# Two phase seams of a fused backward kernel, re-laid: the last output row sums, and the first two rows of the w2 gradient

## The chip, the cores and the metric

The kernel runs on one core of a Trainium2 chip. The metric is the device time of one execution in microseconds (us), the median of several runs. Five engines work side by side, each through its own queue in order: TensorE (PE, matmuls), VectorE (DVE), ScalarE (ACT), GpSimd (POOL) and SyncE (SP), the last used here only to issue DMA transfers; POOL issues transfers as well.

## The reference, cut to what matters

The reference is the forward pass of a block and all its gradients (a vector-Jacobian product with `grad_out`). The block takes tokens `x` (2048 x 1024), normalizes and modulates them, mixes them by a two-dimensional FFT with a learned spectrum, normalizes again, and applies an MLP of width 3584:

```python
def _B_ref(x, w1, b1, w2, b2):
    y = _layernorm(x, axis=-1)
    h = _gelu(jnp.einsum('bsd,df->bsf', y, w1) + b1)
    return jnp.einsum('bsf,fd->bsd', h, w2) + b2
x = A_x
mod = (_silu(c) @ w_mod).reshape(c.shape[0], 6, 1, -1)
sa, ca, ga, sb, cb, gb = (mod[:, 0].copy(), ..., mod[:, 5].copy())
h = _layernorm(x, axis=-1) * (1 + ca) + sa
x = x + ga * _A_ref(h, A_w_r, A_w_i)
h = _layernorm(x, axis=-1) * (1 + cb) + sb
x = x + gb * _B_ref(h, B_w1, B_b1, B_w2, B_b2)
return x
...
_out, _vjp = jax.vjp(_f, A_x, A_w_r, A_w_i, B_w1, B_b1, B_w2, B_b2, c, w_mod)
_grads = _vjp(grad_out)
```

Three results matter here. The gradient of `gb` is the sum over all tokens of `grad_out` times the MLP's output; it is the last of six rows that feed the gradient of `w_mod`. The gradient of the MLP's input is the product of the gradient before the activation with `w1` transposed. The gradient of `w2` is the product of the hidden activations, transposed, with `grad_out * gb`, summed over tokens.

## The kernel before, in words

The kernel works through phases, one after another on TensorE, and the tile framework plans the order of each engine's queue ahead of time: it goes by the order in the program, by when it expects inputs and buffers to be ready, and by the marks `tc.high_priority()` (sooner) and `tc.issue_after(ins)` (the instructions of this block that run on the engine of `ins` stand behind it). Buffers with one tag share a place: a later tile of the tag waits until the earlier one is no longer read. PSUM has eight banks of 128 x 512, in three pools: `ps_s` (two banks), `ps_d` (two) and `ps_f` (four).

**The forward MLP** (lines 762 to 881) runs over four blocks of 512 tokens (`b`), in an order written out by hand (`plan`). `z_block` makes the hidden activations and their gradient factors and stores them to `d_hh` and `d_gz`. `bo_pass(b, h)` makes one column half `h` of the output of a block: 112 matmuls into four banks (`pbo`), evictions on ACT, then on DVE the product `go * bo` and the output itself (`otile` holds these, and the tag is `ot`). After that it yields, and its remainder sums the product over tokens: four `pa` matmuls, added by DVE to `gacc`. The last pass, b = 3 and h = 1, keeps its sums in `ps_s` and `ps_d`; its remainder runs right behind the plan (lines 879 and 880), and `store_gmod` (line 881) writes `gacc` to the DRAM row 5 of `d_gmod`.

**The input gradient** (lines 977 to 1030) runs over the same blocks. For each, SP loads `n3u`, `n2u`, the tokens of `grad_out` into `got` (tag `ot`, half of it by POOL's indirect loads) and seven groups of `d_gz` into a ring of eight slots (`gzr`). For each column half, 112 `pg` matmuls go into the four `ps_f` banks, seven weight groups of sixteen. ACT evicts them, and a chain on DVE and ACT (`ln_bwd`, products, sums, `fold_tok`, `fold_d`) makes that block's part of `fbuf2`. Column sums of intermediate results go to TensorE again (`sums3`, `sums3_ga`, into `acc3`). The ring `early` works the row 5 of the modulation gradient through in eight steps: load a block of `w_mod`, two DVE instructions, store; its first `next` loads the row from `d_gmod` and the first two blocks of `w_mod`.

**The w2 gradient** starts behind it. Four tiles `gB0` to `gB3` hold `grad_out` of a token block each, scaled by `gb` on DVE; they take the places of the weight tiles `w1T_0` to `w1T_3`. `pieces()` is a generator whose steps are spread over later phases by `fill(n)`. For each of 28 rows `fc` of 128 hidden channels it loads the activations by a transposing DMA (`hh_load`), and for each column half adds up 16 matmuls, four on each `gB`, into one `ps_f` bank:

```python
        hh_load(0)
        yield
        hh_load(1)
        for fc in range(NFC):
            if fc + 2 < NFC:
                hh_load(fc + 2)
            for h in range(2 if fc < NFC - 2 else 0):
                acc = ps_f("gw2acc")
                for t in range(NT):
                    gw2_mm(acc, fc, h, t)
                gw2_out(acc, fc, h)
                yield
```

Lines 1173 to 1179 run sixteen of these steps ahead of the spectral backward pass: the first `next` issues row 0's load, then `fill(6)` stands behind the last `gB` load on SP, then come the last block's column sums (`sums3(3, ...)`) and `fill(10)`. The spectral pass then begins with `s_fwd` (the `pu` matmuls), which reads all four parts of `fbuf2`.

Of the kernel before, what the change touches and what calls it, by code (L numbers as in the profile page):

```python
# [11 lines left out]
BF16 = mybir.dt.bfloat16  # L12
I32 = mybir.dt.int32
ACT = mybir.ActivationFunctionType
ALU = mybir.AluOpType
AX = mybir.AxisListType

P = 128
S = 2048
D = 1024  # L20
# [3 lines left out]
NFC = F // P  # L24
KH = D // 2
# [5 lines left out]
NB = 4  # L31
# [4 lines left out]
def kernel(  # L36
# [89 lines left out]
    def load_tok(t4, src, i, eng=None):  # L126
        s3 = tok_flat(src)
        ins = (eng or nc.sync).dma_start(out=t4[:, 0:4:3, :],
                          in_=bass.AP(tensor=s3.tensor, offset=s3.offset + 128 * i * D, ap=[[D, P], [1024 * D, 2], [1, D]]))
        for q in range(2):  # L130
            nc.gpsimd.indirect_dma_start(out=t4[:, 1 + q, :], out_offset=None, in_=s3,
                                         in_offset=bass.IndirectOffsetOnAxis(ap=xidx[:, 2 * i + q:2 * i + q + 1], axis=0))
        return ins
# [38 lines left out]
    def tt(out, a, b, op):  # L172
        return nc.vector.tensor_tensor(out=out, in0=a, in1=b, op=op)  # L173

    def store_gmod(srcs, r):
        row = small.tile([1, D], BF16, tag="gmrow", bufs=1)
        for h in range(2):
            nc.vector.tensor_copy(out=row[:, h * KH:(h + 1) * KH], in_=srcs[h])
        nc.sync.dma_start(out=d_gmod[r * D:(r + 1) * D].rearrange("(o n) -> o n", o=1), in_=row[:])
# [623 lines left out]
    def bo_pass(b, h):  # L803
        cs_ = slice(h * KH, (h + 1) * KH)
        pbs = [(ps_f if b < NB - 1 or h == 0 else (ps_s, ps_d)[k % 2])("pbo") for k in range(4)]
        for i in range(4):
            with ordered():
                last_pe[0] = nc.tensor.matmul(pbs[i][:], lhsT=ones_bf[0:1, :], rhs=b2_row[0:1, cs_], start=True, stop=False)
        for g in range(7):
            wp = w2p[w2n[0] % 4]  # L810
            w2n[0] += 1
            nc.sync.dma_start(out=wp, in_=w2_v[:, g * 4:(g + 1) * 4, cs_])
            hh = hh_slots[(b * 7 + g) % 11]
            for i in range(4):
                for k in range(4):
                    with ordered():
                        last_pe[0] = nc.tensor.matmul(pbs[i][:], lhsT=hh[:, k, i * P:(i + 1) * P], rhs=wp[:, k, :],  # L817
                                                      start=False, stop=(g == 6 and k == 3))
            if g < 6:
                yield  # L820
        bo, x1t, go = (otile[0][:, k] for k in range(3))
        nc.sync.dma_start(out=x1t, in_=chunk_rows(d_x1, b)[:, :, cs_])
        load_tok_half(go, grad_out, b, h)
        for i in range(4):
            with tc.high_priority():
                last_ev[0] = nc.scalar.copy(out=bo[:, i, :], in_=pbs[i][:])
        tt(go, go, bo, ALU.mult)
        tt(bo, bo, bcn(gb_row[:, cs_], 4), ALU.mult)
        tt(bo, bo, x1t, ALU.add)
        store_tok_half(out_0, bo, b, h)  # L830

        yield
        pa = (ps_d if b < NB - 1 else ps_f)("pa")
        for i in range(4):
            with ordered():
                last_pe[0] = nc.tensor.matmul(pa[:], lhsT=ones_bf[:], rhs=go[:, i, :], start=(i == 0), stop=(i == 3))
        with tc.high_priority():
            if b == 0:
                nc.vector.tensor_copy(out=gacc[:, cs_], in_=pa[0:1, :])  # L839
            else:  # L840
                tt(gacc[:, cs_], gacc[:, cs_], pa[0:1, :], ALU.add)
# [19 lines left out]
    for kind, b, g in plan:  # L861
# [7 lines left out]
        else:  # L869
# [6 lines left out]
                bo_late.clear()  # L876
            if g == 13:
                next(boq[b], None)
    for late in bo_late:
        next(late, None)  # L880
    store_gmod([gacc[:, 0:KH], gacc[:, KH:D]], 5)

    gb1 = small.tile([P, NFC], FP32, tag="gb1", bufs=1)
    nc.vector.reduce_sum(out=gb1[:], in_=gb1_acc[:], axis=AX.X)
    gb1_bf = small.tile([P, NFC], BF16, tag="b1_bf", bufs=1)
# [67 lines left out]
    n3u = reg.tile([P, 4, D], BF16, name="n3u", tag="uv1")  # L953
    n2u = reg.tile([P, 4, D], BF16, name="n2u", tag="uv2")
    pru = reg.tile([P, 4, D], BF16, name="pru", tag="uv3")[:]
    got = reg.tile([P, 6, D], BF16, name="got", tag="ot")
    fbuf2 = reg.tile([P, 4, 4, D], BF16, name="fbuf2", tag="fr")
    acc3 = [ps_d("acc3a"), ps_d("acc3b")]
    gzn = 0
    gmw = reg.tile([P, 2, D], BF16, name="gmw", tag="ph")  # L960
    gmg = reg.tile([P, 2, D], BF16, name="gmg", tag="sb")
    early = gmod_ring((5,), [gmw[:, 0], gmw[:, 1], gmg[:, 0]], gmg[:, 1, :])
    next(early)
    au = reg.tile([P, 4, D], BF16, name="au", tag="px1")

    fold2_in = {}

# [9 lines left out]
    for b in range(NB):  # L977
        gn3 = gn3s[b % 2]
        sums = small.tile([P, 2, 4], FP32, tag="sums")
        gzt = []  # L980
        nc.sync.dma_start(out=n3u[:], in_=chunk_rows(d_n3, b))
        nc.sync.dma_start(out=n2u[:], in_=chunk_rows(d_x1, b))
        norm_act(n2u, n2u, 1, b)
        go4 = got[:, 0:4, :]
        load_tok(go4, grad_out, b)
        for g in range(7):
            sl = gzr[gzn % 8 // 2][:, gzn % 2]
            gzn += 1
            nc.sync.dma_start(out=sl, in_=d_gz_v[:, g * 4:(g + 1) * 4, b * BW:(b + 1) * BW])
            gzt.append(sl)  # L990
        for h in range(2):
            pgs = [ps_f("pg") for _ in range(4)]
            for g in range(7):
                for i in range(4):
                    for k in range(4):
                        nc.tensor.matmul(pgs[i][:], lhsT=gzt[g][:, k, i * P:(i + 1) * P],  # L996
                                         rhs=w1Ts[g][:, k, h * KH:(h + 1) * KH],
                                         start=(g == 0 and k == 0), stop=(g == 6 and k == 3))
            for i in range(4):
                with tc.high_priority():  # L1000
                    nc.scalar.activation(out=gn3[:, i, h * KH:(h + 1) * KH], in_=pgs[i][:], func=ACT.Identity,
                                         accum_out=sums[:, h, i:i + 1])
        tt(sums[:, 0, :], sums[:, 0, :], sums[:, 1, :], ALU.add)
        for i in range(4):
            t = 4 * b + i
            ln_bwd(gn3[:, i, :], sums[:, 0, i:i + 1], n3u[:, i, :], stats[:, 2, 0, t:t + 1], gn3[:, i, :], got[:, 4 + i % 2, :])
        next(early, None)
        tt(pru, gn3[:], n2u[:], ALU.mult)
        g2, ftmp = gn3, pru
        if b < NB - 1:  # L1010
            sums3(b, gn3, pru)
        else:
            g2, ftmp = gn3s[0], gzr[0].rearrange("p a b (c d) -> p (a b c d)", c=1).rearrange("p (q d) -> p q d", d=D)
        s2c = small.tile([P, 4], FP32, tag="s2c")
        for i in range(4):
            t = 4 * b + i
            nc.vector.tensor_tensor_reduce(out=g2[:, i, :], in0=gn3[:, i, :], in1=opcb_row, scale=1.0, scalar=0.0,
                                           op0=ALU.mult, op1=ALU.add, accum_out=s2c[:, i:i + 1])
            ln_bwd(g2[:, i, :], s2c[:, i:i + 1], n2u[:, i, :], stats[:, 1, 0, t:t + 1], g2[:, i, :], got[:, 4 + i % 2, :])
        next(early, None)  # L1020
        tt(g2[:], g2[:], go4, ALU.add)
        nc.gpsimd.dma_start(out=chunk_rows(d_gx1, b), in_=g2[:])
        nc.sync.dma_start(out=au[:], in_=chunk_rows(d_A, b))
        tt(n3u[:], g2[:], bcn(ga_row, 4), ALU.mult)
        fold_tok(n3u, ftmp)
        fold2_in[b] = fold_d(fbuf2[:, b], n3u[:], ftmp)
        tt(au[:], g2[:], au[:], ALU.mult)
        if b < NB - 1:
            sums3_ga(b, au)
            next(early, None)  # L1030
# [58 lines left out]
    def gw2_mm(acc, fc, h, t):  # L1089
        nc.tensor.matmul(acc[:], lhsT=hh_s[hh_o[fc]][:, t, :], rhs=gBs[t // 4][:, t % 4, h * KH:(h + 1) * KH],  # L1090
                         start=(t == 0), stop=(t == NT - 1))
# [21 lines left out]
    def pieces():  # L1113
        def hh_load(fc):
            hh_in[0] = nc.sync.dma_start_transpose(out=hh_s[hh_o[fc]], in_=d_hh[fc * P:(fc + 1) * P, :])

        hh_load(0)
        yield
        hh_load(1)
        for fc in range(NFC):  # L1120
            if fc + 2 < NFC:
                hh_load(fc + 2)
            for h in range(2 if fc < NFC - 2 else 0):
                acc = ps_f("gw2acc")
                for t in range(NT):
                    gw2_mm(acc, fc, h, t)
                gw2_out(acc, fc, h)
                yield
# [39 lines left out]
    def fill(n):  # L1168
        for _ in range(n):
            next(todo)  # L1170
        done[0] += n

    next(todo)
    with tc.issue_after(gb_in.ins):
        fill(6)
    for cl in (CE, SE, CO, SO):
        nc.sync.dma_start(out=(smA2, smB2)[cl % 2][:, cl // 2], in_=d_SF[:, cl])
    sums3(3, gn3s[1], pru)
    fill(10)
    nc.sync.dma_start(out=em2, in_=d_E[:, 0])  # L1180

    def mid_bwd():
# [74 lines left out]
```

## Time and profile before

| what | value |
|---|---|
| median of 4 runs | 1523.47 us (1519.96 to 1535.19) |
| profiled execution, its own time | 1524.67 us |
| profiled execution, span | 1522.5 us |
| TensorE busy | 1433.5 us (94%), 6697 matmuls |
| DVE busy | 1073.1 us (70%) |
| ACT busy | 722.5 us (47%) |
| POOL busy | 363.4 us (24%) |
| mean granted TensorE clock | 0.982 |
| DRAM traffic | 324.27 MB by DMA, mean 213 GB/s |

The profile comes from one execution. Its own time holds the span (first to last instruction) and what lies around it. Engine shares are averages over the whole span. The granted clock is the share of its full clock that TensorE was given. In listings by order of time, a line has the start in us, the length in us, the engine, the program line, the operation, the output and inputs, and in brackets how long the engine was idle before and what ended that. SPq is the queue of DMA issues on SP; the length there is the time of the issue, not of the transfer.

### The profile page before, as it was taken

What the parts mean: (1) busy time and instruction counts of PE and PEld (TensorE: products, weight loads), DVE (VectorE), ACT (ScalarE), POOL (GpSimd) and SP (SyncE); (2) the same over time, 40 slices, a digit from 0 to 9 for tenths busy, and PEclk for the clock granted to TensorE, in tenths of its full rate; (3) what the DMA queues carried; (4) which work ended last, traced back from release to release, by engine and by line L of the source; (5) the groups of instructions that cost most, each with busy time, mean ns of one, the idle gap of its engine ahead of it and who ended that gap; (6) DMA issues with size and microseconds to landing.
All of it is one profiled execution on the core that took longest, in us unless ns stands there. A gap on an engine that the chain in (4) does not pass through costs nothing.

```text
span 1522.5 us, 18221 instructions
## 1 busy us (share of the span) xinstructions
PE 1433.5 (94%) x6697; PEld 668.7 (44%) x6831; DVE 1073.1 (70%) x1577; ACT 722.5 (47%) x956; POOL 363.4 (24%) x428
## 2 busy tenths in 40 slices
PE   5989899999999999999999999979998899999998
PEld 2434445444444444444434444434444444444443
DVE  5992869897799887877224977967066666898642
ACT  4765556668886666656012333322522344443211
POOL 5720621211113122221111101311033421222422
PEclk9999999999999999999999999989999999999999
DMA  9871744989587886899956336496288986766992
GB/s 327 270 218 42 203 157 160 284 261 340 198 259 243 198 265 232 243 280 263 335 173 213 132 104 221 110 276 174 63 198 225 235 251 174 199 172 165 275 280 103
DMA packets 358160, 324.27 MB, mean 213 GB/s; under 512 B 209187, under 2 KB 300849, under 8 KB 357816
## 3 DMA queue, kind: packets, MB, share of 16 engines
q1 hardware_dynamic: 324184, 207.71, 51.4%
q0 software_dynamic: 33888, 115.41, 22.1%
q8 instruction: 53, 0.87, 0.2%
q14 instruction: 35, 0.29, 0.1%
HBM read 164.15 MB, written 109.10 MB: 179 GB/s over the span
## 4 chain that ended last, share of the span: by engine, by line
PE 50%; DVE 21%; issue 9%; DMA 9%; ACT 6%; POOL 2%; SPq 1%; POOLq 0%; ACTq 0%; DVEq 0%
PE pbo L817 11%; PE gw2acc L1090 10%; PE pz L776 9%; PE pg L996 5%; PE pv L544 4%; DVE ct L173 4%; PE pu L451 3%; PE pp L659 2%; PE gw1acc L1157 2%; DVE got L895 2%; DVE fbuf L173 1%; DMA xt<-d_gx 1%; DMA gB<-in_grad_out_dram 1%; DMA wblk<-in_w_mod_dram 1%; DVE gn3a L900 1%
## 5 line engine op out<-in xcount | busy, mean ns | idle before, releaser
L659 PE MATMUL pp<-gBoT,wt 128*128 128x512 bf16 x874 | 199.0, 381 | 3.2 <-ACT pho L669 1.0
L996 PE MATMUL pg<-w1T,gzr 128*128 128x512 bf16 x884 | 195.8, 380 | 1.1
L1157 PE MATMUL gw1acc<-gzh,n3n 128*128 128x512 bf16 x875 | 195.6, 380 | 1.1
L776 PEld LDWEIGHTS <-w 128*128 128x128 bf16 x896 | 87.6, 98 | 109.0 <-issue 3.6
L996 PEld LDWEIGHTS <-gzr 128*128 128x128 bf16 x896 | 88.0, 98 | 107.6 <-issue 3.1
L659 PEld LDWEIGHTS <-wt 128*128 128x128 bf16 x896 | 87.8, 98 | 104.1 <-issue 3.1
L1157 PEld LDWEIGHTS <-n3n 128*128 128x128 bf16 x896 | 87.8, 98 | 103.8
L776 PE MATMUL pz<-n3Tb,w 128*128 128x512 bf16 x439 | 98.7, 379 | 1.9 <-DVE w2sD L839 1.5
L776 PE MATMUL pz<-n3Ta,w 128*128 128x512 bf16 x440 | 98.2, 379 | 1.9 <-ACT gt L779 1.3
L1090 PE MATMUL gw2acc<-gB,hhsA 128*128 128x512 bf16 x438 | 98.9, 379 | 0.5
L817 PEld LDWEIGHTS <-hhA 128*128 128x128 bf16 x608 | 59.7, 99 | 77.9 <-issue 9.3
L1095 ACT CAST gwo<-gw2acc 128x512 bf16<-128x512 f32 x54 | 30.6, 584 | 121.9 <-PE gw2acc L1090 76.5
L779 ACT ACTIVATE gt<-pz,b_col 128x512 bf16<-128x512 f32 x112 | 72.9, 684 | 29.7 <-PE pz L776 26.0
L785 ACT ACTIVATE gt<-gt 128x2048 bf16<-128x2048 bf16 x28 | 53.4, 1910 | 64.1 <-DVE gt L173 64.0
L173 DVE TENSOR_TENSOR gt<-gt,gt 128x2048 bf16<-128x2048 bf16 x56 | 68.4, 1222 | 15.9 <-ACT gt L787 15.1
L1161 ACT CAST gwo<-gw1acc 128x512 bf16<-128x512 f32 x48 | 27.8, 584 | 108.2 <-PE gw1acc L1157 100.1
L173 DVE TENSOR_TENSOR ct<-ct 128x2048 bf16<-128x2048 bf16 x64 | 76.0, 1219 | 0.8
L1090 PE MATMUL gw2acc<-gB,hht 128*128 128x512 bf16 x250 | 58.4, 391 | 9.6 <-DVE gB L173 9.1
L1090 PEld LDWEIGHTS <-hhsA 128*128 128x128 bf16 x448 | 43.9, 98 | 50.4
L781 ACT ACTIVATE gt<-gt 128x2048 bf16<-128x2048 bf16 x28 | 53.5, 1910 | 7.6 <-DVE gb_acc L796 6.9
L787 ACT ACTIVATE gt<-gt 128x2048 bf16<-128x2048 bf16 x28 | 53.3, 1908 | 0.4
L1162 POOL DMA_DIRECT2D out_dram<-gwo x56 | 30.5, 547 | 86.7 <-ACT gwo L1161 58.5
(314 smaller groups left out, 2552.4 us busy)
## 6 DMA issues: line engine op xcount, KB each, us to landing
gzr<-d_gz SPq DMA_DIRECT2D x28, 512.0 KB, 7.3
wblk<-in_w_mod_dram SPq DMA_DIRECT2D x12, 1024.0 KB, 13.3
d_ph<-pho POOLq DMA_DIRECT2D x21, 512.0 KB, 5.4
out_dram<-otl POOLq DMA_DIRECT2D x40, 256.0 KB, 3.6
d_hh<-hhA POOLq DMA_DIRECT2D x19, 512.0 KB, 5.1
w2sD<-in_B_w_dram SPq DMA_DIRECT2D x14, 512.0 KB, 6.3
hhC<-d_ph SPq DMA_DIRECT2D x14, 512.0 KB, 5.2
w2sA<-d_ph SPq DMA_DIRECT2D x14, 512.0 KB, 5.1
```

Of the source, the lines that this page charges most:

```text
L173: return nc.vector.tensor_tensor(out=out, in0=a, in1=b, op=op)
L544: nc.tensor.matmul(pv[:], lhsT=R[:, cl * 4 + m, :, :].rearrange("p x w -> p (x w)")[:, base:base + 255:2], rhs=smi[:, cl // 2, m, :], star ...
L659: last_pe[0] = nc.tensor.matmul(pp[:], lhsT=wt[:, fg % 2, cch, k * P:(k + 1) * P], rhs=gBoT[j][:, cch, :], start=(cch == 0), stop=(cch == ...
L776: last_pe[0] = nc.tensor.matmul(pz[:], lhsT=w1s[g][:, cch, k * P:(k + 1) * P], rhs=n3T[:, cch, :], start=(cch == 0), stop=(cch == NDC - 1))
L779: nc.scalar.activation(out=zb[:, k, :], in_=pz[:], func=ACT.Identity, bias=b1_col[:, fc:fc + 1], scale=1.0)
L781: nc.scalar.activation(out=av, in_=zb, func=ACT.Square)
L785: nc.scalar.activation(out=sg, in_=bv, func=ACT.Sigmoid, scale=2.0 * GK)
L787: nc.scalar.activation(out=bv, in_=bv, func=ACT.Sigmoid, scale=-2.0 * GK)
L817: last_pe[0] = nc.tensor.matmul(pbs[i][:], lhsT=hh[:, k, i * P:(i + 1) * P], rhs=wp[:, k, :], start=False, stop=(g == 6 and k == 3))
L996: nc.tensor.matmul(pgs[i][:], lhsT=gzt[g][:, k, i * P:(i + 1) * P], rhs=w1Ts[g][:, k, h * KH:(h + 1) * KH], start=(g == 0 and k == 0), sto ...
L1090: nc.tensor.matmul(acc[:], lhsT=hh_s[hh_o[fc]][:, t, :], rhs=gBs[t // 4][:, t % 4, h * KH:(h + 1) * KH], start=(t == 0), stop=(t == NT - 1))
L1157: nc.tensor.matmul(acc[:], lhsT=n3ns[t // 4][:, t % 4, cch * P:(cch + 1) * P], rhs=gz2[t // 8][:, t % 8, :], start=(t == 0), stop=(t == NT ...
```

## The change: what it does

At the first seam, the remainder of the last `bo_pass`, the store of row 5, the first step of `early` and the tiles `got` and `au` move from before the input gradient to between the matmuls of its first half (b = 0, h = 0) and that half's evictions. The load of `got` for block 0 moves with them. The last `pa` uses the pool `ps_s` instead of `ps_f`.

At the second seam, rows 0 and 1 of the w2 gradient are made together, token block by token block, with four accumulators in two pools. The load of row 1 is issued before the first yield, and the column sums of the last block come after eight pieces instead of six.

```diff
-        pa = (ps_d if b < NB - 1 else ps_f)("pa")
+        pa = (ps_s if b == NB - 1 and h == 1 else ps_d if b < NB - 1 else ps_f)("pa")
...
-    for late in bo_late:
-        next(late, None)
-    store_gmod([gacc[:, 0:KH], gacc[:, KH:D]], 5)
-
...
-    got = reg.tile([P, 6, D], BF16, name="got", tag="ot")
...
-    next(early)
-    au = reg.tile([P, 4, D], BF16, name="au", tag="px1")
...
-        go4 = got[:, 0:4, :]
-        load_tok(go4, grad_out, b)
+        if b > 0:
+            load_tok(got[:, 0:4, :], grad_out, b)
...
+            if b == 0 and h == 0:
+                for late in bo_late:
+                    next(late, None)
+                store_gmod([gacc[:, 0:KH], gacc[:, KH:D]], 5)
+                next(early)
+                got = reg.tile([P, 6, D], BF16, name="got", tag="ot")
+                au = reg.tile([P, 4, D], BF16, name="au", tag="px1")
+                load_tok(got[:, 0:4, :], grad_out, b)
...
-        tt(g2[:], g2[:], go4, ALU.add)
+        tt(g2[:], g2[:], got[:, 0:4, :], ALU.add)
...
         hh_load(0)
+        hh_load(1)
         yield
-        hh_load(1)
         for fc in range(NFC):
             if fc + 2 < NFC:
                 hh_load(fc + 2)
-            for h in range(2 if fc < NFC - 2 else 0):
+            if fc == 1:
+                first = [(f_, h, (ps_s, ps_f)[f_]("gw2acc")) for f_ in range(2) for h in range(2)]
+                for b in range(NB):
+                    for f_, h, acc in first:
+                        for t in range(4 * b, 4 * b + 4):
+                            gw2_mm(acc, f_, h, t)
+                    if b < NB - 1:
+                        yield
+                for f_, h, acc in first:
+                    gw2_out(acc, f_, h)
+                yield
+            for h in range(2 if 1 < fc < NFC - 2 else 0):
...
     with tc.issue_after(gb_in.ins):
-        fill(6)
+        fill(8)
...
     sums3(3, gn3s[1], pru)
-    fill(10)
+    fill(8)
```

## The prediction

> **What bounds the kernel now.** I read the page first, then the table of who waited for whom on TensorE over 700 to 1100 us, then the order of time on each engine at the two places the change touches, then the stretches there.
>
> ```profile
> span 1522.5 us, 18221 instructions
> PE 1433.5 (94%) x6697; PEld 668.7 (44%) x6831; DVE 1073.1 (70%) x1577; ACT 722.5 (47%) x956; POOL 363.4 (24%) x428
> ```
>
> TensorE is busy for 94% of the span, so time is won only where it stands still or runs slowly. Its waits:
>
> ```profile
> PE gw2acc L1090 <- DVE gB L173: 9.1, 3, 5.1
> PE pa L836 <- DVE otile L173: 3.6, 1, 3.6
> PE acc3a L193 <- DVE au L173: 2.9, 3, 1.0
> ```
>
> The columns are total, times and longest, in us. The two largest are the two seams of the change. Seam one, between the last output pass and the input gradient, in order of time (start, length, engine, line):
>
> ```profile
> 775.26 0.23 PE L188 MATMUL ptr<-fin,gb_bf 128*28 128x128 bf16 x1
> 779.11 1.79 PE L836 MATMUL pa<-otile,ones_bf 128*128 128x512 bf16 x4 [3.62 <-DVE otile L173]
> 780.69 53.14 PE L996 MATMUL pg<-w1T,gzr 128*128 128x512 bf16 x236
> ```
>
> Four column-sum matmuls wait for DVE's product, and the pg matmuls, whose operands are there, stand behind them. Seam two, where the w2 gradient starts:
>
> ```profile
> 997.78 1.03 PE L1090 MATMUL gw2acc<-gB,hht 128*128 128x512 bf16 x4
> 1000.69 1.02 PE L1090 MATMUL gw2acc<-gB,hht 128*128 128x512 bf16 x4 [1.88 <-DVE gB L173]
> 1006.79 1.87 PE L1090 MATMUL gw2acc<-gB,hht 128*128 128x512 bf16 x4 [5.08 <-DVE gB L173]
> 1010.78 3.57 PE L1090 MATMUL gw2acc<-gB,hht 128*128 128x512 bf16 x8 [2.13 <-DVE gB L173]
> 1014.58 16.43 PE L1090 MATMUL gw2acc<-gB,hht 128*128 128x512 bf16 x74 [0.22 <-issue]
> ```
>
> Each arriving token block gives four matmuls of work, then TensorE waits for the next. The blocks come late because of what SP queues and how full the DMA engines are:
>
> ```profile
> 975.13 0.42 SPq L128 DMA_DIRECT2D gB<-in_grad_out_dram  x1
> 975.60 8.22 SPq L1115 DMA_TRANSPOSE hht<-d_hh  x1
> 983.91 0.53 SPq L128 DMA_DIRECT2D gB<-in_grad_out_dram  x1
> 988.12 10.02 SPq L128 DMA_DIRECT2D gB<-in_grad_out_dram  x1
> 998.19 14.36 SPq L1115 DMA_TRANSPOSE hht<-d_hh  x3
> ```
> ```profile
> 1000.00:1010.00 10.00, 2.89 (x8) 0.89 (x8) 4.49 (x3) 0.00 (x0) 1.53 (x1) 0.73 1.13 297
> ```
>
> The last three numbers are granted clock, DMA share and GB/s. The transfers fill the DMA engines, and TensorE runs at clock 0.73 besides waiting.
>
> **Seam one, step by step.** The pa matmuls, DVE's two casts, the row store and the start of the gmod ring move behind the 112 matmuls of the first half (b = 0, h = 0). From the end of ptr (775.49) to the first pg (780.69) are 5.20 us; the four pa come back later at 0.2157 each (112 matmuls of the half take 24.17 us, read from the first evictions of the two halves, 803.44 and 827.61), 0.86. That leaves 4.3. The first half also ran slowly: its first eviction should follow the first pg after 100 matmuls and some 0.2 us, at 802.4, and came at 803.44: 1.0 lost to the clock after the gap. Gain 4.3 to 5.3; I take **5.0**, since no gap is left. The eight gzr loads that pg needs first were issued by 743, and pg's four banks were free. pa takes a bank of pool s, which is idle after ptr, so that edit costs nothing; without it pa would wait for one of pg's four banks.
>
> What is late next: the pa matmuls now end at 775.5 + 24.17 + 0.86 = 800.5. DVE's add and cast wait for them; DVE had only ring steps until 828, so they cover. On SP the moved issues are the row store, the load of the gradient row, the ring's first loads, got and au. In before the row load follows pa's end (780.9) by 4.2 us, so now it comes at 804.7; from that load to the ring's last product took 785.06 to 816.7, 31.6 us, so the ring ends near 836, while DVE's chain for b = 0 starts at 828.3 - 5.0 = 823.3. If every ring step stood ahead of that chain, it and the first column sums behind it on TensorE would be up to 13 us late; if the steps slip into DVE's 7.5 us gap before each later chain (932.7 to 940.2 is one), nothing. The nearest row is TensorE's wait for a DVE product in this stage, 1.0 at most; I take **1.0** and keep 0 and 13. got comes at 801 instead of 796 and is first written as scratch after 823; au is wanted near 860. Seam one: 5.0 - 1.0 = **4.0**.
>
> **Seam two, step by step.** Two rows of the w2 gradient now take four banks together (two of pool s, two of f) and sixteen matmuls per block instead of four. The bound is the last block: its scaling on DVE ends at 1008.44 + 2.29 = 1010.73. Of 256 matmuls in the sixteen pieces and 16 column sums, 48 are then done and 224 remain: 224 x 0.2157 = 48.3, so the first pu could start at 1059.0 instead of 1068.83: 9.8. Against it:
>
> The transpose load of row 1 leaves the block that is held behind the last gB load, and nothing keeps it from following row 0's on SP, ahead of gB 1, 2 and 3, au and n3u. Both rows fill one tile, free at the same moment, and gB 1's slot frees one weight group (16 matmuls, 3.45 us) later. What such a transpose costs there:
>
> ```profile
> L1115 SPq DMA_TRANSPOSE hht<-d_hh x8: 2114/4192/9953, 975.6 to 1046.3; - x8
> ```
>
> 2.1 is the least of the eight issues (min, median, max in ns), 8.2 was row 0's own in this very stretch. The DMA engines are full until 1008, so what goes ahead pushes the rest. I take the median, **4.2**; ends 0 (order unchanged) and 8.2. The clock: in before the eight matmuls after 1010.78 and the wait for the next cost 3.8 instead of 1.7, 2.1 lost. With 4.2 more the gaps become 1001.2 to 1004.8 and 1008.3 to 1010.9, 3.6 and 2.6 us; I take **1.0** between 0 and 2.1. Seam two: 9.8 - 4.2 - 1.0 = **4.6**.
>
> [...] This trace has a shorter gap with a slow run behind it:
>
> ```profile
> 717.73 1.07 PE L808 MATMUL pbo<-b_row,ones_bf 1*128 1x512 bf16 x2 [1.86 <-ACT otile L826]
> 718.73 6.51 PE L817 MATMUL pbo<-w2sD,hhA 128*128 128x512 bf16 x16
> ```
>
> Sixteen matmuls took 6.51 after 1.86 us of idling; the same group takes 3.62 elsewhere. [...]
>
> The covers of seam two. The next stage also needs DVE's last fold, which ends at 1056.60, 45.9 after the last scaling; TensorE arrives 49.3 after it, so DVE keeps 3.4 us of room. DVE's chain waits behind the four scalings in its queue and moves with them. The column sums move from six to eight pieces: pru is ready 17.2 us after the last scaling, TensorE arrives 17.3 to 18.3 after it: no wait; at six they would have waited some 7. The four evictions now come together, 4 x 0.59 on ACT beside a pair of 1.2 us activations: up to 2 us on DVE's chain, inside the 3.4. If DVE gets them, 0.68 each. Row 2's first eviction needs row 0's store (5.1 us landing) and may wait about 1 us, with three other banks free. POOL issues the same stores.
>
> **Sum.** 4.0 + 4.6 = 8.6 us. Behind the first pu, TensorE's gaps end on transfers and DVE work that start from its own progress, and the last 180 us are dense matmuls, so I carry it to the end. The profiled execution took 1524.67 (span 1522.5, 2.2 around it), giving 1516.1; the runs' median is 1523.47, 1.2 less, giving **1515**.
>
> **Rivals.** *The gB loads keep their times.* For it: the planner may hold row 1's transpose until gB 1 is ready, and the busy DMA engines may take a 2.1 us transfer into slack. Against: the shared tile. Seam two then gives 9.8 - 1.0, with seam one's 5.0 unspoilt 13.8: 1523.5 - 13.8 = **1509.7**.
>
> *Seam two gives nothing.* If row 1's transpose stays where it was (its issue took 998.19 to 1008.14, so it landed later still), the first block's row 1 matmuls wait for it and 56 of the 64 come after it; or it costs 8.2 and the clock 2.1. Then only seam one's 4.0 is left: **1519.5**.
>
> *The ring blocks SP: slower.* In before, SP issued all ring loads ahead of the gzr loads that follow the first free slot, which began at 817.09, 32.0 after the row load. If the order is kept, they begin at 804.7 + 32.0 = 836.7, land 7.1 later at 843.8, and the second weight group of b = 1 wants them at 800.5 + 24.17 + 3.45 = 828.1: a stall of 15.7 against 5.0 + 4.6 won, so 1523.5 + 6.1 = **1529.6**. It beats the gains from the point where that first load lands after 837.7. Against it: SP's order follows when things become ready, and these loads become ready at about 804, before the ring's later ones.
>
> **How the numbers follow.** Forecast 0.50 (its own range 1511 to 1519), gB on time 0.22, seam two empty 0.12, ring blocks 0.16. The range reaches from below the second case, 1507, to the slow one, 1529. Faster by over 1% (below 1508.2; 1% is about what a measurement of this kernel can tell from no change) needs both seams whole and the slow clock gone: half of the second case, 0.11. Slower by over 1% (above 1538.7) needs the ring's stall and DVE's lateness added: 0.05. Within 1%: 0.84.
>
> **What would show it.** Right: no wait of pa for otile, pg directly behind ptr, clock 1.0 in 780 to 800; sixteen gw2acc matmuls per gB at seam two, two transposes in a row on SP after the first gB load, the last scaling some 4 us later relative to pg's end; the interval from pg's end to the first pu 4 to 5 us shorter than 71. Wrong: gzr loads issued after 821, pg waiting on a DMA in b = 1, or the first pu waiting for fbuf.

## The result, and the profile after

The changed kernel is a little slower: 1528.44 us median of 52 runs against 1524.15 of 78 runs of the kernel before on the same chips. The ratio is 1.0027, 95% interval 1.0017 to 1.0036: some 4 us lost where 8.6 were forecast as won. The profiled execution took 1523.94, well below its median, so spans are not compared here; stages are.

```profile
span 1522.1 us, 18213 instructions
PE 1425.3 (94%) x6697; PEld 666.4 (44%) x6831; DVE 1071.9 (70%) x1577; ACT 721.2 (47%) x956; POOL 364.0 (24%) x428
```

TensorE has the same 6697 matmuls and the same share of the span. What changed is the list of its waits over 700 to 1100 us (total, times, longest):

```profile
PE acc3a L193 <- DVE gn3a L896: 6.6, 1, 6.6
PE pu L451 <- ACT U L622: 3.8, 1, 3.8
PE gw2acc L1091 <- DMA hht<-d_hh: 3.5, 1, 3.5
PE acc3a L193 <- DVE au L173: 2.5, 3, 1.0
PE ptr L188 <- ACT otile L826: 2.0, 1, 2.0
...
PE gw2acc L1091 <- DVE gB L173: 1.1, 1, 1.1
PE gw2acc L1091 <- ACT gwo L1096: 1.0, 1, 1.0
```

Both waits that the change aimed at are gone or small: pa's 3.6 and most of gB's 9.1. Three new ones, 13.9 us together, stand in their place. The wait of `ptr` is not one of them: in the other twelve profiles it is anything from nothing to 1.0 us, also in kernels that leave the first seam as it was, and it lies ahead of the intervals below. To see what each is worth, four intervals are read from TensorE's order of time in every profile: from the start of `ptr` (end of the forward MLP) to the first `au` column sum of block 0, from there to the first `gw2acc` matmul, from there to the first `pu`, and from there to the first `au` column sum inside the `pu` stage.

| kernel | ptr to au 0 | to gw2acc | to pu | to au 3 | sum, us | ratio to before, 95% interval |
|---|---|---|---|---|---|---|
| before | 92.1 | 130.4 | 71.1 | 13.8 | 307.4 | |
| changed | 95.5 | 128.5 | 67.6 | 19.0 | 310.7 | 1.0027 (1.0017 to 1.0036) |
| seam1_only | 96.9 | 129.0 | 70.9 | 13.8 | 310.6 | 1.0017 (1.0003 to 1.0030) |
| seam2_only | 92.0 | 130.4 | 65.5 | 19.0 | 306.9 | 1.0008 (0.9991 to 1.0025) |
| ring_behind | 86.7 | 140.9 | 72.1 | 17.9 | 317.7 | 1.0058 (1.0036 to 1.0079) |
| ws_behind | 96.6 | 128.9 | 67.1 | 13.8 | 306.4 | 0.9998 (0.9982 to 1.0014) |
| pa_g1_seam1 | 86.7 | 130.9 | 70.5 | 13.8 | 301.9 | 0.9965 (0.9941 to 0.9989) |
| seam1_noring | 86.8 | 130.4 | 68.7 | 13.8 | 299.7 | 0.9961 (0.9940 to 0.9982) |
| seam2_ws | 92.1 | 130.4 | 66.9 | 13.8 | 303.2 | 0.9958 (0.9939 to 0.9978) |
| row0_blocks | 92.1 | 130.4 | 67.5 | 13.8 | 303.8 | 0.9971 (0.9947 to 0.9994) |
| hh1_late | 92.1 | 130.4 | 71.6 | 13.8 | 307.9 | 0.9986 (0.9967 to 1.0005) |
| pa_g1_ws | 86.8 | 130.4 | 66.3 | 13.8 | 297.2 | 0.9945 (0.9922 to 0.9968) |
| row0_pa | 86.8 | 130.4 | 66.6 | 13.8 | 297.6 | 0.9924 (0.9898 to 0.9950) |

The sums come from one execution each, the ratios from many; they agree within 3 us. The changed kernel's stages are 3.3 us longer, and its time some 4 us.

**Seam one.** TensorE in order of time (start, length, engine, line, in brackets the idle time before and what ended it):

```profile
774.69 0.23 PE L188 MATMUL ptr<-fin,gb_bf 128*28 128x128 bf16 x1 [2.00 <-ACT otile L826]
774.85 24.35 PE L989 MATMUL pg<-w1T,gzr 128*128 128x512 bf16 x110
799.04 1.03 PE L836 MATMUL pa<-otile,ones_bf 128*128 128x512 bf16 x4
...
836.45 0.58 PE L193 MATMUL acc3a<-gn3a,sel 128*128 128x512 bf16 x1 [6.60 <-DVE gn3a L896]
```

pg follows ptr at once (5.43 us became 0.16), and pa runs behind the half without a wait. But at 836.45 the first column sum of block 0 has waited 6.6 us. DVE's order of time tells why:

```profile
826.12 1.22 DVE L891 CUSTOM_DVE_ANT_0 got<-gn3a,n3u 128x1024 bf16<-128x1024 bf16 x1
...
829.61 1.23 DVE L930 CUSTOM_DVE_ANT_0 gmw<-gmw,gmg 128x1024 bf16<-128x1024 bf16 x1 [0.87 <-DMA gmw<-in_w_mod_dram]
...
832.39 1.23 DVE L930 CUSTOM_DVE_ANT_0 gmw<-gmw,gmg 128x1024 bf16<-128x1024 bf16 x1 [1.47 <-DMA gmw<-in_w_mod_dram]
...
835.11 2.48 DVE L896 SCALAR_TENSOR_TENSOR gn3a<-gn3a,stats,got 128x1024 bf16<-128x1024 bf16 x2 [0.33 <-ACT got L895]
```

L891 is the chain of block 0, L930 a step of the ring `early`. The last two ring steps stand in the middle of the chain and wait for their loads; the first instruction of the chain also had to wait for the sixth step. The instruction that makes gn3a stands behind them on DVE and began only at 835.11, and TensorE stood. The loss is more than the wait: over the first 2 us behind it (836.40 to 838.40) the granted clock was 0.50.

**Seam two.**

```profile
998.76 1.89 PE L1091 MATMUL gw2acc<-gB,hht 128*128 128x512 bf16 x8
1004.14 5.30 PE L1091 MATMUL gw2acc<-gB,hht 128*128 128x512 bf16 x12 [3.50 <-DMA hht<-d_hh]
...
1013.36 13.97 PE L1091 MATMUL gw2acc<-gB,hht 128*128 128x512 bf16 x63 [1.11 <-DVE gB L173]
...
1066.32 1.89 PE L451 MATMUL pu<-smA,fbuf 128*128 128x512 bf16 x8
1071.98 13.53 PE L451 MATMUL pu<-smA,fbuf 128*128 128x512 bf16 x55 [3.77 <-ACT U L622]
```

After the eight matmuls of row 0 TensorE waits 3.5 us for row 1's transposed load. The first pu comes 67.56 us after the first gw2acc, 3.5 sooner than before, but after eight pu matmuls, two banks full, it waits 3.8 us for ACT, and over 1071.98 to 1074.00 behind that the granted clock was 0.50. SP's queue has the new order:

```profile
976.58 8.02 SPq L1116 DMA_TRANSPOSE hht<-d_hh  x1
984.70 0.53 SPq L128 DMA_DIRECT2D gB<-in_grad_out_dram  x1
985.27 14.42 SPq L1116 DMA_TRANSPOSE hht<-d_hh  x1
...
1001.97 1.58 SPq L128 DMA_DIRECT2D gB<-in_grad_out_dram  x2
```
```profile
1011.01 4.49 DVE L173 TENSOR_TENSOR gB<-gB,rows 128x4096 bf16<-128x4096 bf16 x2 [8.82 <-DMA gB<-in_grad_out_dram]
```

Row 1's transpose stands ahead of the last two gB loads and held SP for 14.4 us. The last scaling of gB (the second of the two in DVE's line) ended at 1015.50, 16.7 after the first gw2acc; before it was 13.0. And this is what ACT waited for when pu stood, on DVE, POOL and ACT:

```profile
1060.29 2.36 DVE L173 TENSOR_TENSOR fbuf<-gzr 128x2048 bf16<-128x2048 bf16 x2
```
```profile
1049.79 0.54 POOL L1098 DMA_DIRECT2D out_dram<-gwo  x1
1062.92 1.01 POOL L470 DMA_INDIRECT ws<-in_A_w_r_dram,xu  x1 [12.60 <-DVE fbuf L173]
...
1067.75 1.16 POOL L1098 DMA_DIRECT2D out_dram<-gwo  x2
```
```profile
1059.34 1.07 ACT L1096 CAST gwo<-gw2acc 128x512 bf16<-128x512 f32 x2 [5.99 <-DMA out_dram<-gwo]
1070.37 1.07 ACT L1096 CAST gwo<-gw2acc 128x512 bf16<-128x512 f32 x2 [9.96 <-DMA out_dram<-gwo]
```

Three gwo stores stand on POOL behind the ws loads, and those wait until DVE's last fold has released their buffer. POOL's order of these was the same in before, where the last load and the first store behind it were:

```profile
1060.76 0.96 POOL L470 DMA_INDIRECT ws<-in_A_w_i_dram,xu  x1 [0.30 <-issue]
1061.71 0.59 POOL L1097 DMA_DIRECT2D out_dram<-gwo  x1
```

Only the times moved. The fold ended at 1062.65 instead of 1056.60 while TensorE came sooner; the stores went out late, gwo's two slots stayed full, ACT waited 10 us with an eviction, and the evictions of pu stood behind it.

### The profile page after: what moved, and what is told of

Read it like the earlier page. It is cut to its first block, busy times and chain, and to the rows that moved or that the text cites. A ratio compares the mean times of both kernels' runs of the same rounds, so it can differ in the third digit from the quotient of the medians.

```text
span 1522.1 us, 18213 instructions
## 1 busy us (share of the span) xinstructions
PE 1425.3 (94%) x6697; PEld 666.4 (44%) x6831; DVE 1071.9 (70%) x1577; ACT 721.2 (47%) x956; POOL 364.0 (24%) x428
## 4 chain that ended last, share of the span: by engine, by line
PE 44%; DVE 20%; issue 12%; DMA 11%; ACT 6%; POOL 4%; SPq 2%; POOLq 0%; ACTq 0%; DVEq 0%
PE pbo L817 10%; PE pz L776 9%; PE gw2acc L1091 7%; PE pv L544 4%; DVE ct L173 4%; PE pg L989 3%; PE pu L451 3%; PE pp L659 2%; PE gw1acc L1169 2%; DVE got L891 2%; DMA xt<-d_gx 1%; SPq L1116 1%; DVE fbuf L173 1%; DVE gn3a L896 1%; DVE gt L173 1%
```

## The experiments

The theory after the comparison: each seam gives what it should, and a new wait takes it back, on DVE by the ring at seam one, on POOL by the ws loads at seam two. The rivals: all of the loss is one seam's; or the new waits are slack that later stages cover.

**Each seam alone.** `seam1_only` is the changed kernel with `pieces()` and the fills as before; `seam2_only` is the kernel before with the changed `pieces()` and fills.

> The first seam changed, the second as before. Theory (two new waits, one at each seam, eat what the seams give): pg starts some 5 us earlier behind ptr, DVE's ring steps wait for their loads inside the chain of b = 0, TensorE waits about 6.6 us for gn3a, and the w2 gradient starts 1 to 2 us later than before, relative to ptr. Ratio to before 1.001. Rival A (all of the loss belongs to the second seam): no wait for gn3a over 1 us, ratio 0.997. Rival B (all belongs to the first): ratio 1.003.

> The second seam changed, the first as before. Theory: from the end of pg to the first pu about 67.6 us instead of 71.05, then a wait of some 3.8 us of pu for ACT, whose eviction waits for a gwo store; ratio to before 1.001. Rival A (the second seam holds all of the loss): ratio 1.003. Rival B (it holds none): no wait of pu, ratio 0.998.

Measured 1.0017 and 1.0008. The two add up to 1.0025, the change's 1.0027 within their intervals, so neither seam alone is shown to hold all of the loss, and neither gains. Seam one alone has the wait on the ring:

```profile
PE acc3a L193 <- DVE gn3a L896: 7.8, 1, 7.8
```

Its stage to au 0 is 4.8 us longer than before although pg starts 5 us sooner. Seam two alone reaches pu 5.5 us sooner, and loses 5.2 in the pu stage (19.0 instead of 13.8). Its own time can't be told from no change.

**The ws loads behind the stores** (`ws_behind`: the changed kernel, one edit).

```diff
-                nc.gpsimd.indirect_dma_start(out=ws[:, x, 1, 0:DF], ...)
+                with (ExitStack() if fwd or n > 1 else tc.issue_after(gwo_st[0].ins)):
+                    nc.gpsimd.indirect_dma_start(out=ws[:, x, 1, 0:DF], ...)
```

`gwo_st[0]` is the last gwo store ahead of the pu stage (the two lines that set it are left out here). On POOL three stores move ahead of four loads; the rest of its order is kept.

> The changed kernel, with the first two pairs of ws loads on POOL put behind the three gwo stores that stood behind them. Theory: those stores go out some 5 us sooner, ACT's evictions and pu no longer wait, the first sixteen pu run without the gap of 3.8 us, and the total falls by 4 to 5 us: ratio to before 1.000. Rival (the wait of pu is covered by the next stage's transfers): the gap goes, ratio stays at 1.003.

```profile
1059.23 0.54 POOL L1100 DMA_DIRECT2D out_dram<-gwo  x1 [6.37 <-ACT gwo L1098]
1066.14 0.54 POOL L1100 DMA_DIRECT2D out_dram<-gwo  x1 [6.37 <-ACT gwo L1098]
1066.99 1.01 POOL L472 DMA_INDIRECT ws<-in_A_w_r_dram,xu  x1 [0.31 <-issue]
```

The stores wait only for their data, the pu stage is back at 13.8, and the ratio is 0.9998, the changed kernel's loss gone. The same edit on seam two alone (`seam2_ws`):

> The second seam changed, the first as before, with the first two pairs of ws loads on POOL behind the three gwo stores. Theory: the wait of pu for ACT goes, and the second seam gives what is left of it between pg's end and pu, 3 to 4 us: ratio to before 0.998. Rival (the second seam is worth nothing, as the late gB loads and DVE's later fold give it back): ratio 1.000.

Measured 0.9958 (0.9939 to 0.9978) against 1.0008 without the edit: 7.6 us by the ratios, 3.7 by the stages, of which 5.2 are the pu stage and 1.4 go the other way in the stage before it. The second seam is worth 4 to 6 us once the stores are free: 4.2 by the stages, 6.4 by the ratio.

**The ring's steps moved behind the folds** (`ring_behind`).

```diff
+    def ring(b, n):
+        if 0 < b < NB - 1:
+            with tc.issue_after(fold2_in[b - 1].ins):
+                for _ in range(n):
+                    next(early, None)
```

The three calls of `next(early, None)` in the block loop become `ring(b, 1)`, `ring(b, 1)` and `ring(b, 2)`.

> The changed kernel, with the eight steps of the gmod ring put behind the folds of blocks 0 and 1 on DVE. Theory: the wait of TensorE for gn3a of block 0 (6.6 us) goes, the chain of block 0 ends some 8 us sooner relative to ptr, and the total falls by about 6 us against the changed kernel: ratio to before 0.999. Rival (the wait for gn3a is slack that the blocks behind it make up): the wait goes and the ratio stays at 1.003.

The wait of block 0 went as expected (86.7 to au 0), but the kernel became the slowest of all, 1.0058 where 0.999 was expected. Its lines, TensorE and SP:

```profile
889.58 0.58 PE L193 MATMUL acc3a<-gn3b,sel 128*128 128x512 bf16 x1 [4.82 <-DVE gn3b L896]
```
```profile
981.18 22.87 SPq L1122 DMA_TRANSPOSE hht<-d_hh  x2
```

The steps now wait for loads ahead of block 1's chain, 4.8 us, and the planner laid SP out anew: both transposes together behind the second gB load, 22.9 us for the two, for which TensorE waited 10.7. With the ring out of block 0's chain the first wait is gone; put there, a later ring is no cure. What each of the two new losses costs by itself, this run doesn't show.

**The moved part earlier in the half** (`pa_g1_seam1`: `seam1_only`, with the block at `b == 0 and h == 0` behind weight group 1 of 0 to 6).

```diff
-            if b == 0 and h == 0:
+                if b == 0 and h == 0 and g == 1:
```

> The first seam changed, the second as before, and the moved part (pa, the row store, the ring's start, got, au) put after the second of the seven weight groups of the half instead of after the seventh. Theory (the first seam loses because the ring starts 24 us later and its DVE steps wait for loads inside the chain of b = 0): pa still waits for nothing, the ring starts some 17 us sooner and ends before that chain, no wait of TensorE for gn3a over 1 us, and the seam keeps 4 to 5 us: ratio to before 0.997. Rival (the wait for gn3a comes from got and au being loaded later, or the seam's gain is lost anyway in the blocks that follow): ratio 1.000 to 1.002.

Measured 0.9965. The ring's last step and the chain of block 0 on DVE:

```profile
823.97 0.49 DVE L932 TENSOR_SCALAR gmw<-gmg,u_rt 128x1024 bf16<-128x1024 bf16 x1
827.36 1.23 DVE L891 CUSTOM_DVE_ANT_0 got<-gn3a,n3u 128x1024 bf16<-128x1024 bf16 x1 [2.90 <-ACT gn3a L1002]
```

The ring ends 2.9 us before the chain has its input; pa, at 7.1 us behind ptr, still waits for nothing. But got and au also come sooner in this kernel, so the rival on them needed another run.

**The ring left out** (`seam1_noring`: `seam1_only` without the three `next(early, None)` in the block loop; got and au as late as in the change). This kernel leaves out the eight steps' results, the part of the w_mod gradient that row 5 gives, so its time is that of less work (sixteen products on DVE, six loads and eight stores fewer); it is read for the wait and the stage.

> The first seam changed, the second as before, and the eight ring steps left out (the part of the modulation weight gradient of row 5, and that row's share of one vector sum, are not computed); got and au stay as late as in the change. Theory (the ring's waits inside DVE's chain of b = 0 are what the first seam loses by): TensorE's wait for gn3a, 7.8 us with the ring, is under 1 us, and the ratio to before is 0.997 or a little less, for the ring's own work is gone too. Rival (got and au, loaded 5 and 18 us later, hold the chain): a wait of 5 us or more stays, ratio 1.000 or more.

```profile
PE acc3a L193 <- DVE gn3a L896: 0.4, 2, 0.2
```

The wait is gone with got and au late, ratio 0.9961. So it was the ring, not got and au, and the stage to au 0 is the same, within 0.1 us, as with the ring started early.

**What the early transpose costs.** `row0_blocks` is the kernel before with row 0 alone in two `ps_s` banks by token blocks, row 1's load untouched; `hh1_late` is `seam2_ws` with `hh_load(1)` back behind the `yield`.

> The kernel before, with row 0 of the w2 gradient alone made token block by token block (two banks of pool s, eight matmuls for each gB), row 1's load left behind the last gB load. Theory (the transposing load moved ahead of the gB loads is what costs the second seam 4 us): the last scaling of gB keeps its place, 13 us behind pg's end, twelve more matmuls are done by then, and pg's end to the first pu falls by 2 to 3 us with no new wait of pu: ratio 0.998. Rival (the shorter idle time buys nothing, as DVE's fold or the stores then hold pu): ratio 1.000.

> The second seam changed with the ws loads on POOL behind the gwo stores, as in the run with the better ratio (0.9958), but row 1's transposing load back behind the last gB load. Theory (the load must come ahead of the gB loads, for row 1's matmuls of the first block stand in TensorE's queue): the last scaling of gB comes about 13 us after pg's end instead of 15.5, but TensorE waits for the row 1 load until some 14 us after pg's end, and pg's end to the first pu is 69 to 71 us instead of 66.9: ratio 0.998 to 1.000. Rival (the early transpose is pure cost): 65 us or less, ratio 0.995 or less.

Row 0 alone: 0.9971. The last scaling and TensorE behind it:

```profile
1005.54 2.29 DVE L173 TENSOR_TENSOR gB<-gB,rows 128x4096 bf16<-128x4096 bf16 x1 [1.72 <-DMA gB<-in_grad_out_dram]
```

It ended at 1007.83, 12.7 after the first gw2acc, against 15.5 in `seam2_ws`; pu came after 67.5 instead of 71.1, and needed no edit on POOL. With row 1's load late:

```profile
1012.47 28.20 PE L1092 MATMUL gw2acc<-gB,hht 128*128 128x512 bf16 x120 [10.59 <-DMA hht<-d_hh]
```

The last scaling was early as well (1012.28, 12.3 after the first gw2acc), but TensorE stood 10.6 us for row 1, and pu came after 71.6, a little past the 69 to 71 expected. So the early transpose is a price that the two-row form must pay: it costs the gB loads about 3 us, and without it the form gives nothing in its stage. The run's ratio, 0.9986, reaches from 0.9967 to 1.0005 and doesn't tell it from no change.

**Both repairs, and the simpler form.** `pa_g1_ws` is the changed kernel with the moved part behind weight group 1 and the ws loads behind the stores. `row0_pa` has the moved part there, row 0 alone by blocks, and nothing else.

> The changed kernel with both repairs: the moved part after the second weight group, and the first ws loads on POOL behind the three gwo stores. Theory: both gains stand, 4 to 5 us and 3 to 4 us, some 8 us in all: ratio to before 0.995. Rival (each repair only moves the wait to the next queue): ratio 0.998 or more.

> The kernel with the first seam's moved part after the second weight group, and at the second seam row 0 alone by token blocks, row 1's load behind the last gB load. Theory: the two gains measured apart (ratios 0.9965 and 0.9971) add up, some 10 us: ratio 0.994, about that of both repairs on the changed kernel (0.9945), with less moved. Rival (both win back the same idle time): 0.997.

Measured 0.9945 and 0.9924 (0.9898 to 0.9950): both beat the kernel before and the changed one. The gains of the two seams add up in the stages: 5.5 and 3.6 apart, 9.8 together. The simpler form is not shown to be faster than the other, as the intervals overlap; it needs fewer edits.

## Why the prediction was wrong, point by point

The direction was wrong: 1515 forecast, with 1507 to 1529 as the range; the median is 1528.4, near the upper end. That it lies in the range is luck: the upper end stood for a stall of pg behind SP, which did not come.

**Seam one's gain: right.** 4.3 to 5.3 were worked out and 5.0 taken; pg came 5.3 us sooner behind ptr, and the clock was 1.00 over 780 to 800.

**"If every ring step stood ahead of that chain": the failed term.** The working had the place, the mechanism and the end of the range, and then took 1.0 us from TensorE's usual waits for DVE instead of working out where the ring would end. With the ring out of the way the stage to au 0 is 86.75 us, in the change 95.54: 8.8 lost, of which 1.9 came back by the first gw2acc, 6.9 net. The prediction's own figures, ring end near 836 and chain start at 823, spoke for the upper end: in the trace the last ring load's product began at 832.39. The row that gave the 1.0 (TensorE's waits for au, from 867 on) has no ring step ahead of it, so it could not price one. The trace of before had the price: its ring steps waited 8.0 and 3.7 us for their loads, at 804.88 and 813.51, where nothing stood behind them until 828.

**Seam two's terms: the size nearly right, the path not.** The transpose went ahead of the last two gB loads (of three that were named, and of au and n3u); the last scaling came 3.8 later, 4.2 taken. pu came 3.5 us sooner, 4.6 taken. That these are so near is partly luck. The sum went on from the end of the last scaling, but TensorE waited for the third block until 1013.36 and was still at it when the fourth was ready at 1015.50. The wait for row 1's load (3.5), which the sum had at nothing, and the slowed matmuls behind it (12 in 5.30 us, granted clock 0.50) were over by 1012.24, ahead of the third block, so neither was on the path, while the sum took 1.0 for the clock. And a wait of 1.0 that it lacked stands ahead of the column sums: ACT evicted the first four accumulators only from 1026.75 on, behind two activations that had waited for DVE.

**"POOL issues the same stores": the cover that failed.** The working asked what DVE's later fold does to pu, found 3.4 us of room, and pu did start after the fold. It did not ask who else waits for the fold: the ws loads, and on POOL's queue behind them the gwo stores. In before these left at 1061.71 and later, and no eviction of the pu stage was held; in the change they left at 1067.75 and later, which cost 5.2 us in the pu stage.

**The sum by what was measured.** Seam one -5.3 + 6.9 = +1.6; seam two -3.5 + 5.2 = +1.7; together 3.3 us slower where -8.6 was forecast. The signs of being wrong that were named did not come (pg waited for no DMA, pu not for fbuf): none of them was a wait behind the ring on DVE, or for a store on POOL.

**The rivals.** The slower rival had the ring as its cause but SP as its place. There it was wrong: the gzr loads were issued from 804.05, as the argument against it said. "Seam two gives nothing" came out in the total, by neither of its two ways; the first of them, row 1's load left behind, was run (`hh1_late`) and did as described.

**The clock.** The 1.0 us for it at seam two was an estimate, chosen between 0 and the 2.1 lost there in before. In these runs 24 matmuls took 5.35 us behind gaps of 0.9, 1.3 and 1.9 us (`seam2_only`, `ws_behind`, `pa_g1_ws`), and 7.04 behind one of 2.3 (`seam2_ws`). So the matmuls took 1.7 us longer behind one gap, and not behind three shorter ones. The row that the prediction showed, a gap of 1.86 us and then 16 matmuls in 6.51 (granted clock 0.55 over 718.73 to 725.24), is not as plain: before has another gap of 1.86 us, at 750.13, and the 15 matmuls behind it took 3.61, at clock 1.00 over 750.13 to 753.50. What makes the difference, no run here shows.

## What to carry to other kernels

When work moves later, follow its longest dependent chain to its end and ask what stands behind each of its links in an in-order queue: an engine that looks idle where the work lands can still hold the next chain for a load (here DVE stood 0.87 and 1.47 us for the last two ring loads, and TensorE 6.6 for gn3a). A cover must be checked for every waiter on the thing that becomes late, not only for the one that comes to mind; here the fold's second waiter was a load on POOL, with stores behind it. And the smaller form of an idea, one row instead of two, or a few matmuls of cover instead of a whole half, can win as much, since 7.1 us of cover (`pa_g1_seam1`) sufficed for a wait of 3.6 (pa in before).

## What was not expected of the hardware

In the changed kernel the issue of one transposing load held SP's queue for 14.4 us (985.27), where the DMA engines were full (share 1.10 over 985 to 1000), while the least of eight in before took 2.1; the next issue on SP came at 999.80, and the last two gB loads at 1001.97. Executions of the same kernel lay between 1516 and 1535 us over 78 runs, so that a single profiled time said nothing about a change of 4 us; the stage intervals agreed between kernels to 0.1 us wherever their queues were alike (13.8 in ten of the thirteen, 130.4 in eight).
